# Issuing full matmuls as 32-column PE tiles in a fused attention and feed-forward kernel

## The chip, the cores and the metric

The kernel runs on one core of a Trainium2 chip. The metric is the device time of one execution in microseconds. The profile's span is about 1.8 us shorter than that time. "TensorE" is the matmul engine (PE in the profile, PEld its weight loads), VectorE is DVE, ScalarE is ACT, GpSimd is POOL.

## The reference

Eight batches of 12 heads, 448 tokens, head size 64, go through attention with one added to the softmax's denominator; the result, as 3584 rows of 768, goes through a feed-forward layer that takes the elementwise maximum of three up projections.

```python
scores = (1.0 / np.sqrt(64)) * np.matmul(q, k.transpose(0, 1, 3, 2))
m = np.max(scores, axis=-1, keepdims=True)
e = np.exp(scores - m)
attn = e / (np.sum(e, axis=-1, keepdims=True) + np.exp(-m) + 1e-09)
x = np.matmul(attn, v)            # then (8, 448, 12, 64) -> (3584, 768)
h = np.maximum(np.maximum(x @ w1, x @ w2), x @ w3)
out = h @ w_out
```

## The kernel before

Four heads make a group, three groups a batch. The groups' scores, exponentials and AV products are woven into the feed-forward pieces of the batch before, so that TensorE always has work. The first batch goes in halves of 224 query columns (`scores_half`, `av_half`, `up_half`), so that the feed-forward can begin early; all others use 448 columns. These are the matmuls that the change touches, and the AV product that it does not touch:

```python
def scores_visit(i, units):                        # L187; scores_half (L260) is the same with 224 columns
    ...
        for hh in range(2):
            nc.tensor.matmul(
                out=stp[:, hh, 0:S],
                lhsT=qkT[hh * D : hh * D + D, c * SC : c * SC + 128],   # 64 rows x 128 columns
                rhs=qkT[hh * D : hh * D + D, S : 2 * S],
                start=True, stop=True)

def up_piece(b, fc, i):                            # L325; up_half (L344) is the same with 224 columns
    ...
    for dc in range(NDC):
        nc.tensor.matmul(out=p_i[:, 0:S], lhsT=w_sb[i][:, dc, ts(fc, 128)],
                         rhs=xT[b][:, dc, :], start=(dc == 0), stop=(dc == NDC - 1))

def out_piece(bp, t, nh):                          # L366
    ...
    for fc in range(NFC):
        nc.tensor.matmul(out=op_ps[:, 0:NW], lhsT=hT[bp][:, fc, ts(t, 128)],
                         rhs=wout_sb[:, fc, ts(nh, NW)], start=(fc == 0), stop=(fc == NFC - 1))

# av_group (L216) and av_half (L286): already 32-column tiles, one head each
            for c in range(NCH):
                for hh in range(GH):
                    nc.tensor.matmul(out=bank[32 * hh : 32 * hh + 32, 0:S], lhsT=weights(hh, c),
                                     rhs=eT[:, hh, c, :], start=(c == 0), stop=(c == NCH - 1))
```

Each matmul call becomes two instructions, a weight load and a matmul (3148 of each in the profile of before). The loads of q, k, v and of the four weight matrices are issued by GpSimd; the weights and the first eight groups' inputs are fetched in the first 60 us.

The softmax here doesn't subtract the row's maximum and nothing guards it: scores larger than these inputs give would overflow.

## Time and profile before

| | before |
|---|---|
| time, median of 2 runs | 360.17 us (359.98 to 360.36) |
| span of the profiled run, mean granted clock | 358.9 us, 0.999 |
| TensorE busy | 95%, 3148 matmuls and as many weight loads |
| VectorE, ScalarE busy | 59%, 54% |
| chain that ended last | 91% of it matmuls |
| DMA engines' busy share, 18 to 62 us | 1.27 (mean of 16 engines; over 1 means packets overlap) |

"Busy" for TensorE uses modelled ends of matmuls, so the distance between starts is the better measure. Three views carry the argument, and the prediction shows their lines: the page, and two stretches of TensorE's timeline. A timeline line has the start in us, the length in us, the engine, the line of the kernel, the operation and its tiles, partitions times columns, and how many records were merged.

### The profile page before, as it was taken

To read this page: it belongs to the slowest core of one execution; us is meant where nothing else is said; L and a number is where in the kernel's file an instruction comes from. 1 tells how busy PE (TensorE), PEld (TensorE's weight loads), DVE (VectorE), ACT (ScalarE), POOL (GpSimd) and SP (SyncE) were. 2 spreads that over 40 slices of the span, in tenths; PEclk is the share of its full clock that TensorE was granted. 3 is DMA by queue.
4 is the path that set the end of the run, shared out by engine and by line. 5 is a ranking of instruction groups with operands and counts; after the bars stand their busy time and mean duration, and the time that the engine had idled before them with its cause. 6 is when DMAs were issued, how large, how long until landed. Compare 5 with 4: busy or idle time off the path is not lost.

```text
span 358.9 us, 7470 instructions
## 1 busy us (share of the span) xinstructions
PE 341.4 (95%) x3148; PEld 178.2 (50%) x3148; DVE 213.4 (59%) x430; ACT 192.7 (54%) x247; POOL 58.1 (16%) x90
## 2 busy tenths in 40 slices
PE   3879899999999999999999999999999999999994
PEld 2557777544444444444444544444445444445552
DVE  3334566676666666665657657656656655656553
ACT  3697567875563664663762863763764664630000
POOL 8424532220220220220220220220000000000000
PEclk9999999999999999999999999999999999999999
DMA  9999999489746964857739876759421540012006
GB/s 137 193 208 206 202 199 161 59 171 162 102 66 124 179 125 75 118 107 161 103 57 122 150 166 101 102 99 188 53 54 26 136 118 2 0 46 88 2 4 173
DMA packets 71617, 40.75 MB, mean 114 GB/s; under 512 B 33824, under 2 KB 66848, under 8 KB 71584
## 3 DMA queue, kind: packets, MB, share of 16 engines
q0 software_dynamic: 35072, 21.01, 42.9%
q1 hardware_dynamic: 36272, 19.05, 22.2%
q8 instruction: 24, 0.39, 0.4%
q10 hardware_dynamic: 240, 0.23, 0.2%
q14 instruction: 9, 0.07, 0.1%
HBM read 42.47 MB, written 11.01 MB: 149 GB/s over the span
## 4 chain that ended last, share of the span: by engine, by line
PE 91%; ACT 2%; DVE 2%; DMA 2%; issue 1%; POOL 1%; DVEq 0%; POOLq 0%
PE p_i L325 41%; PE op_ps L366 15%; PE av L216 15%; PE stp L187 11%; PE p_i L344 6%; DMA ld_k<-in_k_dram 2%; PE trT L157 2%; ACT eTh L269 1%; PE stp L260 1%; PE num L286 1%; PE den L286 1%; ACT rb L302 0%; DVE xT L308 0%; ACT lnd L298 0%; DVE qkT L162 0%
## 5 line engine op out<-in xcount | busy, mean ns | idle before, releaser
L196 ACT ACTIVATE eT<-stp 112x896 f16<-112x896 f32 x168 | 141.9, 912 | 109.3 <-PE stp L187 109.3
L335 DVE TENSOR_TENSOR hT<-hT,p_i 128x448 f16<-128x448 f16 x84 | 52.2, 622 | 43.5 <-PE p_i L325 43.5
L366 PE MATMUL op_ps<-w_130,hT 128*128 128x384 f16 x336 | 57.9, 327 | 0.0
L325 PE MATMUL p_i<-xT,w_127 128*128 128x448 f16 x252 | 54.7, 353 | 0.0
L325 PE MATMUL p_i<-xT,w_129 128*128 128x448 f16 x252 | 54.6, 353 | 0.0
L325 PE MATMUL p_i<-xT,w_128 128*128 128x448 f16 x252 | 54.6, 353 | 0.0
L89 POOL DMA_DIRECT2D ld_v<-in_v_dram x24 | 17.0, 709 | 177.0 <-PE stp L187 171.8
L366 PEld LDWEIGHTS <-hT 128*128 128x128 f16 x336 | 31.6, 98 | 25.1 <-issue 3.0
L187 PE MATMUL stp<-qkT 64*128 64x448 f16 x336 | 42.7, 353 | 0.0
L373 DVE TENSOR_SCALAR o_sb<-op_ps 128x384 f32<-128x384 f32 x56 | 31.1, 556 | 18.4 <-PE op_ps L366 18.4
L216 PE MATMUL av<-eT,ld_v 112*32 112x448 f16 x672 | 38.8, 353 | 0.0
L333 DVE CAST hT<-p_i 128x448 f16<-128x448 f32 x42 | 26.2, 625 | 20.8 <-PE p_i L325 20.8
L325 PEld LDWEIGHTS <-w_127 128*128 128x128 f16 x252 | 23.6, 98 | 25.2 <-issue 4.4
L325 PEld LDWEIGHTS <-w_129 128*128 128x128 f16 x252 | 23.9, 98 | 24.7 <-issue 3.3
L325 PEld LDWEIGHTS <-w_128 128*128 128x128 f16 x252 | 23.9, 98 | 24.7 <-issue 3.3
L231 DVE COPY num<-av 128x448 f32<-128x448 f32 x42 | 26.2, 625 | 8.8 <-PE av L216 6.0
L269 ACT ACTIVATE eTh<-stp 112x896 f16<-112x896 f32 x24 | 20.5, 912 | 12.7 <-PE stp L260 12.6
L216 PEld LDWEIGHTS <-ld_v 112*32 112x32 f16 x672 | 18.6, 97 | 16.5 <-issue 5.0
L240 DVE TENSOR_TENSOR xT<-num,rb 128x448 f16<-128x448 f32 x42 | 25.9, 617 | 0.0
L187 PEld LDWEIGHTS <-qkT 64*128 64x128 f16 x336 | 11.3, 94 | 24.6 <-issue 19.1
L226 DVE COPY den<-av 128x448 f32<-128x448 f32 x21 | 13.1, 625 | 16.1 <-PE av L216 16.1
L216 PE MATMUL av<-eT,ones_121 112*32 112x448 f16 x336 | 19.8, 355 | 0.0
(161 smaller groups left out, 225.6 us busy)
## 6 DMA issues: line engine op xcount, KB each, us to landing
ld_v<-in_v_dram POOLq DMA_DIRECT2D x24, 224.0 KB, 4.1
ld_q<-in_q_dram POOLq DMA_DIRECT2D x23, 224.0 KB, 5.1
ld_k<-in_k_dram POOLq DMA_DIRECT2D x23, 224.0 KB, 6.1
out_dram<-o_sb SPq DMA_DIRECT2D x8, 336.0 KB, 3.0
out_dram<-o_sb SPq DMA_DIRECT2D x8, 288.0 KB, 3.8
out_dram<-o_sb SPq DMA_DIRECT2D x8, 240.0 KB, 3.4
out_dram<-o_sb SPq DMA_DIRECT2D x8, 192.0 KB, 2.7
w_127<-in_moe_w_dram POOLq DMA_DIRECT2D x3, 384.0 KB, 11.9
```

The costliest lines, as they stand in the source:

```text
L187: nc.tensor.matmul(out=stp[:, hh, 0:S], lhsT=qkT[hh * D : hh * D + D, c * SC : c * SC + 128], rhs=qkT[hh * D : hh * D + D, S : 2 * S], sta ...
L196: nc.scalar.activation(out=st["eT"][:, 2 * pr : 2 * pr + 2, c, :], in_=stp[0:SC, :, 0:S], func=AF.Exp, scale=scale,)
L216: nc.tensor.matmul(out=bank[32 * hh : 32 * hh + 32, 0:S], lhsT=weights(hh, c), rhs=eT[:, hh, c, :], start=(c == 0), stop=(c == NCH - 1),)
L231: nc.vector.tensor_copy(out=num[:, hf], in_=col_tiled(lambda hh, c: v16[:, hh, c, hf::2])[:, 0:S])
L240: nc.vector.tensor_tensor(out=xT[b][:, 2 * g + hf, :], in0=num[:, hf], in1=rb, op=ALU.mult)
L269: nc.scalar.activation(out=st[key][:, 2 * pr : 2 * pr + 2, 2 * n : 2 * n + 2, :], in_=stp[0:SC, :, 0:S].rearrange("p h (c q) -> p h c q", ...
L325: nc.tensor.matmul(out=p_i[:, 0:S], lhsT=w_sb[i][:, dc, ts(fc, 128)], rhs=xT[b][:, dc, :], start=(dc == 0), stop=(dc == NDC - 1),)
L333: nc.vector.tensor_copy(out=dst, in_=p_i[:, 0:S])
L335: nc.vector.tensor_tensor(out=dst, in0=dst, in1=p_i[:, 0:S], op=ALU.max)
L344: nc.tensor.matmul(out=p_i[:, ts(j, HQ)], lhsT=w_sb[i][:, dc, ts(2 * fp + j, 128)], rhs=xT[b][:, dc, ts(half, HQ)], start=(dc == 0), stop= ...
L366: nc.tensor.matmul(out=op_ps[:, 0:NW], lhsT=hT[bp][:, fc, ts(t, 128)], rhs=wout_sb[:, fc, ts(nh, NW)], start=(fc == 0), stop=(fc == NFC - 1),)
L373: nc.vector.tensor_scalar(out=o_sb[:, ts(nh, NW)], in0=op_ps[:, 0:NW], scalar1=1.0 / LAMBDA, scalar2=None, op0=ALU.mult,)
```

## The change

The matmuls of five functions go through a helper that cuts the stationary operand into strips of 32 columns and issues one matmul for each strip. The output lands in the same place, in four strips of 32 partitions. The intent is to use one kind of column tile throughout, as the AV product does; the products to compute are the same. (`CT = 64`, used in one experiment, is this helper with another constant.)

```diff
+    CT = 32
+
+    def mm(out, lhsT, rhs, start, stop):
+        m = lhsT.shape[-1]
+        for j in range(0, m, CT):
+            nc.tensor.matmul(
+                out=out[j : j + CT],
+                lhsT=lhsT[:, j : j + CT],
+                rhs=rhs,
+                start=start,
+                stop=stop,
+            )
+
@@ scores_visit, scores_half, up_piece, up_half, out_piece
-                nc.tensor.matmul(
+                mm(
... (the same one-line edit in each of the five)
```

## The prediction

> **What bounds the kernel now.** I read the page from the top: busy shares, the slices, the chain that ended last, then the groups, and last the timeline of TensorE.

> ```profile
> PE 341.4 (95%) x3148; PEld 178.2 (50%) x3148; DVE 213.4 (59%) x430; ACT 192.7 (54%) x247; POOL 58.1 (16%) x90
> ...
> PE   3879899999999999999999999999999999999994
> ...
> PEclk9999999999999999999999999999999999999999
> ...
> q8 instruction: 24, 0.39, 0.4%
> ...
> PE 91%; ACT 2%; DVE 2%; DMA 2%; issue 1%; POOL 1%; DVEq 0%; POOLq 0%
> PE p_i L325 41%; PE op_ps L366 15%; PE av L216 15%; PE stp L187 11%; PE p_i L344 6%; DMA ld_k<-in_k_dram 2%; PE trT L157 2%; ACT eTh L269 1%; PE stp L260 1%; PE num L286 1%; PE den L286 1%; ACT rb L302 0%; DVE xT L308 0%; ACT lnd L298 0%; DVE qkT L162 0%
> ```

> TensorE is full from slice 5 (36 us) to the end, at full clock, and 91% of the chain is matmuls. VectorE (59%) and ScalarE (54%) have room. So what counts is the distance from one matmul's start to the next. It can't be read from the mean of a group (353 ns for a 448-column matmul, an end that is modelled); it is read from starts in the timeline:

> ```profile
> 151.35 1.30 PE L325 MATMUL p_i<-xT,w_129 128*128 128x448 f16 x6
> 152.48 2.19 PE L366 MATMUL op_ps<-w_130,hT 128*128 128x384 f16 x12
> ...
> 155.28 0.94 PE L216 MATMUL av<-eT,ones_121 112*32 112x448 f16 x16
> 156.05 1.85 PE L216 MATMUL av<-eT,ld_v 112*32 112x448 f16 x32
> ```

> Six full up-projection matmuls take 152.48 - 151.35 = 1.13 us, 188 ns each. The AV product is already written as 32-column tiles, four to a round (one per head): 16 of them take 156.05 - 155.28 = 0.77 us, 192 ns for a round of four. In the single records a round has its four starts 2 to 5 ns apart and the next round begins 189 ns after the first (the median over all rounds of AV; full matmuls of L325: 189 ns too). A round of four 32-column tiles costs what one full matmul costs. The first phase, which works in halves of 224 columns, says the same at half the length:

> ```profile
> 30.04 0.57 PE L286 MATMUL den<-eTh,ones_121 112*32 112x224 f16 x16
> 30.43 0.94 PE L286 MATMUL num<-eTh,ld_v 112*32 112x224 f16 x32
> 31.30 0.56 PE L260 MATMUL stp<-qkT 64*128 64x224 f16 x8
> 31.79 1.32 PE L344 MATMUL p_i<-xT,w_128 128*128 128x224 f16 x12
> 33.05 0.81 PE L260 MATMUL stp<-qkT 64*128 64x224 f16 x8
> 33.78 0.57 PE L286 MATMUL den<-eTh,ones_121 112*32 112x224 f16 x16
> 34.18 0.94 PE L286 MATMUL num<-eTh,ld_v 112*32 112x224 f16 x32
> 35.05 0.57 PE L157 MATMUL trT<-ident_102,qk_641 112*128 112x112 f16 x8
> ```

> 16 small ones from 30.04 to 30.43: 0.39 us, 97 ns a round; single records give 96 ns for a round of four and 96 ns for one full 224-column matmul of L344.

> [...] rounds of four overlap as above, and the first start after a change between the forms of L325, L187 and L216 comes about 285 ns after the last one, not 189, so a change costs about 95 ns. [...] The 32-column loads of AV show no cost: four of them hide in a round of 96 ns. [...] 24 packets, 0.39 MB, for some 6,300 instructions.

> **The change part by part.** It removes 1,740 full-width matmuls with their weight loads: 756 (L325), 336 (L366), 336 (L187), 216 (L344), 96 (L260). It puts four times as many in: 6,960. AV (1,008 and 288) and the 112 transposes stay. Matmuls go from 3,148 as recorded (3,148 by this sum) to 8,368, so loads and matmuls together from 6,296 to 16,736. The order of the work, the waits (on the first matmul of a chain only) and the other engines' instruction lists are the same in both kernels; I compared the lists.

> Array time. L325: 756 rounds, 189 ns against 189: 0. L366: 384 columns, 162 ns against 162 by the same rule, 336 rounds: 0. Scores: two heads already run side by side (starts 4 ns apart, pairs 189 to 199 ns apart), and become eight tiles in place of two; if they too overlap, each pair gains 6 more starts of about 3 ns only in its tail. The last of four starts some 10 ns after the first, so each chain ends 10 ns later for its reader; on a full TensorE this is no time, and where TensorE waits, in the first 36 us, some 30 such waits are 0.3 us. [...] Sum of the array's part: within 0.5 us of zero.

> Supply of instructions. This is where I chose. Each round now eats 8 instructions (4 loads, 4 matmuls) where it ate 2. I counted the starts of before in 10 us stretches and multiplied them: 120 to 320 us would need 9,080 instructions in 200 us, one per 22.0 ns; 20 to 60 us need 696, 696, 744 and 624, one per 14.5 ns; 60 to 80 us 554 and 478. What can TensorE's sequencer deliver? The lines of the first phase above show 16+32+8+12+8+16+32 = 124 matmuls, 248 instructions, between 30.04 and 35.05, without a gap that isn't a wait. [...] Call the delivery time r. A stretch that needs n instructions takes n times r if that is over its 10 us. Summing the excess:
> r = 14 ns or less: about 0.5 us.
> r = 16.7 ns [...]: 1.6 + 1.6 + 2.4 + 0.4 = 6 us, all in the first 60 us.
> r = 20 ns: 3.9 + 3.9 + 4.9 + 2.5 + 1.1 = 16 us.
> r = 25 ns: 35 us before 80 us and (12,208 x 25 ns - 270 us) = 35 us from 80 to 350 us, 70 us in all.
> Fetching the instructions themselves: 16,736 at 64 bytes are 65 blocks; one takes 0.9 to 1.5 us in the trace, and a block lasts 256 x 22 ns = 5.6 us (3.7 us in the first phase). If the next block is asked for at the start of this one, it comes in time.

> **Rivals.**
> (a) Nothing happens: the array is the bound[...]. For it: the AV chains, which are this very form, keep 189 and 96 ns to their last round, in runs of 96 instructions. [...] Time 360 to 361 us.
> (b) The sequencer becomes the bound in the half-column first phase only, where a round lasts 96 ns and needs 8 instructions in it (12 ns each): 366 to 376 us.
> (c) It becomes the bound everywhere: scores need 16 instructions in 189 ns, out rounds 8 in 162 ns (20 ns each), up rounds 8 in 189 ns (24 ns each). [...] Against it: inside a round, starts are 2 to 5 ns apart with loads between. 400 to 430 us.
> (d) Faster, since TensorE would change form less often. [...] some 120 changes of 95 ns would give 11 us back. Nothing in before shows it: 112x32 beside 64x128 pays the full 95 ns.
> (e) Eight score tiles that do not all overlap: if they ran as two rounds, 216 pairs (168 of 189 ns, 48 of 96) would cost 36 us more. Against it: the pairs of row tiles and the rounds of column tiles each overlap in before.

> **Range and chances.** I give (a) about half, (b) a quarter, (c) and (e) together 0.2, (d) 0.03. The 2% line is 7.2 us, so the slow end of (a) and the quick end of (b), up to r = 17 ns, still count as the same. The middle lies at r of about 16.7 ns, 366 us; the range reaches from (a) at its best, 359 us, to r of about 23 ns, 400 us. Faster 0.03, same 0.52, slower 0.45.

> **What would show it.** In the profile of after: rounds of up at 189 ns, out at 162 ns and scores at 189 ns with four or eight starts some 3 ns apart mean (a). Starts spread evenly, 2r apart, in the chains of the half phase alone, mean (b), and the first op_ps start, at 68.1 us now, comes later by what is lost; in all chains, (c). Scores at twice their length beside up rounds of 189 ns mean (e); first starts after a change of form at 189 and not 285 ns, (d). The instruction queue should show about 64 packets; if gaps of a microsecond stand before blocks, fetching is the bound, which I hold for unlikely. The prediction is wrong if the time leaves 359 to 400 us, and its reasoning is wrong, whatever the time, if the rounds at full supply are not 189 ns.

## The result, and the profile after

The changed kernel took 381.66 us (median of 2 runs, 380.27 and 383.06) against 360.17 us: slower, at a ratio of 1.060 (95% interval 1.043 to 1.077). Ratios here are the mean time of one kernel's fast runs over that of the other's in the same rounds, so they aren't quite the ratio of the medians quoted.

The page of the changed kernel, the same lines as were shown of before. All changed matmuls now have the helper's line, L135:

```profile
PE 349.2 (92%) x8368; PEld 201.7 (53%) x8368; DVE 213.6 (56%) x430; ACT 192.9 (51%) x247; POOL 58.1 (15%) x90
...
PE   3767577999999999999999999999999999999994
...
PEclk9998889999999999999999999999999999999999
...
q8 instruction: 65, 1.06, 1.2%
...
PE 86%; ACT 5%; issue 4%; DVE 2%; DMA 2%; POOL 1%; DVEq 0%; POOLq 0%
PE p_i L135 44%; PE op_ps L135 14%; PE av L229 13%; PE stp L135 11%; ACT eT L209 2%; DMA ld_k<-in_k_dram 2%; PE trT L170 2%; ACT eTh L282 2%; PE num L299 1%; PE den L299 1%; DVE xT L321 0%; DVE qk L156 0%; ACT rb L315 0%; ACT rb L250 0%; DVE qkT L175 0%
```

The counts are as worked out: 8368 matmuls, 65 instruction packets. From slice 8 on the row of TensorE is all nines, as before. The difference lies in slices 2 to 7, the first 66 us: TensorE has holes, and in slices 4 to 6 the granted clock falls (to 0.8 in the row PEclk). In the chain "issue" grows from 1% to 4%: time in which an engine waited for nothing that the profile shows. The view of waits (engine and line, what it waited for, us in total, times, longest) puts it on TensorE:

```profile
PE p_i L135 <- issue: 8.5, 5, 3.0
...
PE den L299 <- issue: 2.7, 1, 2.7
...
PE stp L135 <- issue: 0.8, 2, 0.5
...
PE trT L170 <- issue: 0.5, 1, 0.5
```

These are 12.5 us in nine waits for issue; in before the same view lists none. The timeline shows where they stand, in the middle of a chain of matmuls that has all its inputs:

```profile
33.15 0.95 PE L135 MATMUL p_i<-xT,w 128*32 128x224 f16 x31
35.28 0.64 PE L135 MATMUL p_i<-xT,w 128*32 128x224 f16 x17 [1.19 <-issue]
...
37.51 0.95 PE L135 MATMUL p_i<-xT,w 128*32 128x224 f16 x31
41.48 0.64 PE L135 MATMUL p_i<-xT,w 128*32 128x224 f16 x17 [3.02 <-issue]
```

```
block k  its first instruction  gap before it  packet of block k+1 starts   packet k+1 to block k+1's start
   3           23.44 us             0.78 us    27.12 us  (3.68 us later)      2.24 us
   4           29.36                2.07       32.95     (3.59)               2.33
   5           35.28                1.45       39.03     (3.75)               2.45
   6           41.48                3.28       45.10     (3.62)               2.30
   7           47.40                0.81       51.17     (3.77)               2.43
   8           53.59                2.97       54.73     (1.14)               not starved
   9           58.34                none       61.59     (3.25)               2.21
  10           63.80                2.16       64.93     (1.13)               not starved
```

So in these eight rows one block is fetched ahead: the packet of the next one starts only after TensorE has entered a block. It starts 3.6 to 3.8 us later in the first 50 us, 1.1 us later at 53.6 and at 63.8 us, and 3.25 us later at 58.3 us; from its start another 2.2 to 2.5 us pass until TensorE runs on. The view by windows shows what differs; the last three numbers of a line are the granted clock, the DMA engines' busy share and GB/s:

```profile
30.00:32.00 2.00, 2.00 (x52) 1.92 (x48) 0.63 (x1) 0.00 (x0) 0.86 (x2) 0.50 1.08 212
38.00:40.00 2.00, 0.46 (x19) 0.20 (x12) 0.02 (x1) 1.18 (x2) 1.40 (x2) 1.00 1.45 199
62.00:64.00 2.00, 0.20 (x9) 0.20 (x12) 0.00 (x0) 1.24 (x2) 0.00 (x0) 1.00 0.00 0
```

At 38 us the DMA engines are saturated (1.45) with the loads of weights and inputs; at 62 us they are idle. At 58 us, where the packet was late again, the share was 1.44 (58 to 60 us); from 54 to 56 us it was 0.25. What the packet waits for, no run shows. A block thus takes about 3.7 + 2.3 = 6.0 us while they are saturated, 23.5 ns an instruction, and 1.1 + 2.3 = 3.4 us while they are idle, 13.3 ns an instruction. Before used up a block in 7.4 to 10.5 us in that phase, so its fetches, whose packets start late as well (2.0 to 3.1 us after the block, up to 50 us), were hidden.

The first line shows the second loss. Three times, for 3.4 us each, the granted clock was 0.50: from 29.3, 43.0 and 53.2 us on, each within 1.5 us of the end of a gap of 2.1 us or more. The gap's length alone does not decide: after the gap of 2.16 us that ends at 63.80 us the clock stayed full. In the traces of before and after the clock holds one value for multiples of 3.41 us (3.41, 6.83, 10.24, 13.65, 320.85 and 341.33 us; the last piece of each trace apart). Counted on that grid, TensorE was busy for 1.24, 1.49 and 1.09 us in the stretch before these three falls, and for 1.86 us in the one from 60.03 to 63.44 us. Of the 201 stretches at full clock in which matmuls ran in these two traces, the three were the only ones with less than 1.86 us busy, and the only ones followed by a fall. From 29.36 us, 65 small matmuls (16.25 rounds of 96 ns, 1.6 us) took 3.3 us; the other two times cost 1.1 and 1.4 us by the same count.

The sum: I compared the starts of ScalarE's 246 activations, which are the same in both kernels. The changed kernel is 17.8 us behind by the 57th (65 us in before), and from there to its end only 1.8 us more, 19.6 us in all. The 17.8 us are 12.3 of the 12.5 us of waits (0.2 us come later) and some 4.2 us of lowered clock; the remaining 1.3 us I didn't attribute. The later 1.8 us are one late block at 232 us (0.65 us) and a steady drift of 1.2 us, which two experiments below place.

The steady part is otherwise what the array's arithmetic said. A stretch of the changed kernel:

```profile
168.44 2.45 PE L135 MATMUL p_i<-xT,w 128*32 128x448 f16 x48
170.72 2.22 PE L135 MATMUL op_ps<-w,hT 128*32 128x384 f16 x48
...
173.57 0.94 PE L229 MATMUL av<-eT,ones 112*32 112x448 f16 x16
174.33 1.84 PE L229 MATMUL av<-eT,ld_v 112*32 112x448 f16 x32
```

48 small matmuls, which stand for 12 full ones, take 170.72 - 168.44 = 2.28 us, 190 ns a round. The median of rounds inside chains is 189 ns (448 columns), 163 ns (384), 96 ns (224), and 199 ns for a pair of scores, to the nanosecond what full matmuls took.

### The profile page after: what moved, and what is told of

Read it like the earlier page. It is cut to its first block, busy times and chain, and to the rows that moved or that the text cites. A ratio compares the mean times of both kernels' runs of the same rounds, so it can differ in the third digit from the quotient of the medians.

```text
span 378.5 us, 17910 instructions
## 1 busy us (share of the span) xinstructions
PE 349.2 (92%) x8368; PEld 201.7 (53%) x8368; DVE 213.6 (56%) x430; ACT 192.9 (51%) x247; POOL 58.1 (15%) x90
## 4 chain that ended last, share of the span: by engine, by line
PE 86%; ACT 5%; issue 4%; DVE 2%; DMA 2%; POOL 1%; DVEq 0%; POOLq 0%
PE p_i L135 44%; PE op_ps L135 14%; PE av L229 13%; PE stp L135 11%; ACT eT L209 2%; DMA ld_k<-in_k_dram 2%; PE trT L170 2%; ACT eTh L282 2%; PE num L299 1%; PE den L299 1%; DVE xT L321 0%; DVE qk L156 0%; ACT rb L315 0%; ACT rb L250 0%; DVE qkT L175 0%
## 5 line engine op out<-in xcount | busy, mean ns | idle before, releaser
L135 PE MATMUL p_i<-xT,w 128*32 128x448 f16 (+1 forms) x3888 | 175.8, 336 | 9.2 <-issue 8.5
L135 PEld LDWEIGHTS <-w 128*32 128x32 f16 x3888 | 101.9, 98 | 81.4 <-issue 24.9
L135 PE MATMUL op_ps<-w,hT 128*32 128x384 f16 x1344 | 58.1, 327 | 0.0
L135 PE MATMUL stp<-qkT 64*32 64x448 f16 (+1 forms) x1728 | 52.8, 339 | 4.7 <-DVE qkT L175 2.9
L135 PEld LDWEIGHTS <-hT 128*32 128x32 f16 x1344 | 40.6, 97 | 16.2 <-issue 2.8
L135 PEld LDWEIGHTS <-qkT 64*32 64x32 f16 x1728 | 18.1, 92 | 31.6 <-issue 23.9
L229 PE MATMUL av<-eT,ones 112*32 112x448 f16 x336 | 19.7, 355 | 0.0
L89 POOL DMA_DIRECT2D ld_q<-in_q_dram x24 | 17.0, 707 | 4.0 <-DMA w<-in_moe_w_dram 1.4
L89 POOL DMA_DIRECT2D ld_k<-in_k_dram x24 | 16.8, 701 | 2.6 <-DMA w<-in_moe_w_dram 1.1
L248 ACT ACTIVATE lnd<-den,one_b 128x448 f32<-128x448 f32 x21 | 14.3, 679 | 4.3 <-DVE den L239 4.3
## 6 DMA issues: line engine op xcount, KB each, us to landing
w<-in_moe_w_dram POOLq DMA_DIRECT2D x9, 384.0 KB, 12.5
```

Of the source, the lines that this page charges most:

```text
L89: nc.gpsimd.dma_start(out=tiles[name][:, h0 : h0 + step].rearrange("p h c d -> p h (c d)"), in_=src[:, h0 : h0 + step],)
L135: nc.tensor.matmul(out=out[j : j + CT], lhsT=lhsT[:, j : j + CT], rhs=rhs, start=start, stop=stop,)
L248: nc.scalar.activation(out=lnd, in_=den, func=AF.Ln, bias=one_b)
```

## The experiments

Theory A, formed from this trace: the blocks of instructions come too slowly where the DMA engines are saturated. Rivals: B, TensorE's sequencer can't decode more than one instruction in some 20 ns, whatever the DMA engines do; C, the form itself costs a little in every round; D, the lowered clock is the cause and not a consequence.

Twelve kernels ran, in four lots, each beside runs of before on the same chip (medians of before there: 360.73, 361.12, 360.67 and 360.80 us).

### Only the first phase tiled

`half_only`: `scores_visit`, `up_piece` and `out_piece` call `nc.tensor.matmul` again; the two half functions keep `mm`.

```diff
-                mm(              # in scores_visit, up_piece, out_piece
+                nc.tensor.matmul(
```

> Only the two half-column functions of the first phase (scores_half, up_half) issue 32-column tiles. Theory A (instructions of TensorE come in blocks of 256; the next block is asked for when the last one is begun, and while the DMA engines are saturated a block takes about 6 us from the start of one to the start of the next, 23 ns an instruction): the loss lies where many instructions meet saturated DMA engines, so most of it stays: +12 to +17 us on before, with idle gaps of TensorE put down to issue at every 256th instruction. Theory B (the sequencer decodes too slowly, whatever the DMA engines do): the same place and about the same time, but the starts stretched evenly inside a block. Theory C (a round of 32-column tiles costs a little more everywhere): the loss follows the number of tiled matmuls, 312 of 1740, +4 us.

377.41 us (376.12 to 379.03, 4 fast runs), ratio 1.046 (1.042 to 1.050): +16.7 us. Its waits:

```profile
PE p_i L135 <- issue: 7.0, 4, 3.0
...
PE den L299 <- issue: 3.0, 1, 3.0
```

All breaks are again after 191 modulo 256 instructions. By the 57th activation it is 17.9 us behind the profiled run of before, and that stays 17.9 to 18.0 us to the last activation: no drift at all. Theory C's +4 us is out.

### Only the full-column work tiled

`full_only`, the complement.

```diff
-                mm(              # in scores_half, up_half
+                nc.tensor.matmul(
```

> Only scores_visit, up_piece and out_piece issue 32-column tiles; the first phase is as before. Theory A: the full-column work needs one instruction per 22 ns, and its blocks come in 3.4 us when the DMA engines are not saturated, so it is hidden but for small ends: +1 to +3 us. Theory B, with a sequencer slow enough to cost 18 us in the first phase (20 ns an instruction): out and score rounds would be bound, but the average is not: +1 to +4 us. Theory C: 1428 of 1740 tiled matmuls, +15 us.

362.56 us (361.70 to 366.10, 7 fast runs), ratio 1.004 (1.002 to 1.006): +1.8 us, with no wait put down to issue. 1428 of the 1740 tiled matmuls cost half a per cent, 312 cost the rest. It is where the instructions fall, not how many there are.

### Full-column scores alone, and up and out projections alone

`scores_only` keeps `mm` in `scores_visit` only, `ffn_only` in `up_piece` and `out_piece` only (the edit is the same one line in the other functions).

> Only the full-column scores (scores_visit) issue 32-column tiles: eight tiles of 64 rows in place of two of 128 columns. In the trace of the change the steady part lags before by 1.2 us more at its end than at its beginning. If the eight starts of a pair (about 3 ns apart) make each of the 63 visits end some 14 to 20 ns later, it is +1 us (ratio 1.002 to 1.004). If the lag belongs to the feed-forward or to single late blocks of instructions, 0 (ratio 0.999 to 1.001).

362.05 us against 360.67 us (22 and 43 runs), ratio 1.004 (1.002 to 1.006). In its trace the lag grows evenly, by 0.98 us between the activations that start at 56 and 310 us in before. With 63 visits of scores in 21 groups, that is about 16 ns a visit. The starts show where: inside a visit two pairs of scores stay 199 ns apart, as in before, but from the last pair to the first matmul of the up projection after it are 305 ns, where before has 285. The 20 ns more are the time between the first and the last of the eight starts.

> Only the full-column up and out projections (up_piece, out_piece) issue 32-column tiles. Rounds of four took as long as one full matmul in the trace of the change, so 0 to +0.5 us (ratio 0.999 to 1.002). If a round of four cost even 1% more, 756 x 1.9 ns + 336 x 1.6 ns = +2 us (ratio 1.005).

361.50 us, ratio 1.001 (0.999 to 1.004): no difference that 22 runs could show. Its trace is 0.4 us behind at the last activation, of which 0.25 us are one step at 251 us. So most of the drift of the change belongs to the scores.

### Fewer loads in the first phase

`before_now` and `after_now` fill the weights by a memset on GpSimd in place of loading them; the results are wrong on purpose. The pair is compared with each other.

```diff
-            nc.gpsimd.dma_start(out=w_sb[i][:, 2 * g : 2 * g + 2, :], in_=src)
+            nc.gpsimd.memset(w_sb[i][:, 2 * g : 2 * g + 2, :], 1.0 / 64.0)
```

> Control, wrong result on purpose: before with the four weight matrices filled by a memset in place of their 12 loads, so that the DMA engines carry less in the first 60 us. All theories: 355 to 361 us, as TensorE hardly waits for weights in before.

380.49 us (377.81 to 381.23, 4 fast runs): the control missed its expectation by 20 us. TensorE waits 23.1 us for VectorE's copies of q and k, most of it near the beginning, where before waits 6.5 us. The trace shows how: one copy of q, 0.3 us long in most places, lasts 14.5 us, from 7.3 to 21.9 us, while GpSimd runs nine of the memsets (8.4 to 21.7 us), and a copy of k lasts 4.0 us beside the last three. The phase that matters, from 30 us on, is undisturbed.

> Wrong result on purpose: after with the same memset of the weights, to be compared with before_now. Theory A: with the DMA engines no longer saturated from about 30 us on, a block of instructions takes about 3.4 us (13 ns an instruction) and most gaps go: after_now minus before_now is 3 to 8 us in place of 20 to 21. Theory B (decode): the instructions are the same, so the difference stays 17 to 21 us. Theory D (the lowered clock is the cause and not a consequence of the gaps): the clock still falls to 0.83 between 40 and 60 us and the loss stays.

389.65 us (388.07 to 391.54, 4 fast runs): 9.2 us more than its control, where the unaltered pair differs by 20 to 21 us; the runs of either kernel spread by 3.4 us. Less than half of the loss is left, though more than the 3 to 8 us that I expected. The trace tells why it is not less: the loads of q, k and v still saturate the engines from 54 to 62 us (shares of 1.17 to 1.44) and from 68 to 70 us (1.40), and there the packets again start 3.1 to 3.7 us after the block, and the two largest gaps are 2.4 and 2.7 us; between 46 and 52 us, where the share is 0.03, the blocks follow each other in 3.6 to 3.7 us with packets 0.9 to 1.1 us after the block. Its waits for issue, 6.7 us in place of 12.5, and the view of those six microseconds:

```profile
PE p_i L135 <- issue: 3.4, 5, 2.1
PE den L299 <- issue: 2.4, 1, 2.4
PE stp L135 <- issue: 0.9, 1, 0.9
...
46.00:52.00 6.00, 5.62 (x247) 4.63 (x240) 2.41 (x5) 3.54 (x6) 0.50 (x1) 1.00 0.03 5
```

The mean clock is 0.992 to 1.000 in the four runs. Theory B, which expected 17 to 21 us, is out. So is D: gaps appear here, and in the change from 23.4 us on, before any fall of the clock.

### The rate of instructions measured by itself

`burst` is before with matmuls on a scratch bank that wait for nothing, 512 in the first phase and 1024 at the end.

```diff
+    def burst(nb):
+        scratch = ps1.tile([128, 512], FP32, tag="bank1", name="burst")
+        for n in range(nb):
+            j = 32 * (n % 4)
+            nc.tensor.matmul(out=scratch[j : j + 32, 0:32], lhsT=ident16[:, j : j + 32],
+                             rhs=ident16[:, 0:32], start=True, stop=True)
```

> Before, with two stretches of matmuls on a scratch bank added, each matmul of 32 columns by 32, four column tiles in turn, nothing to wait for: 512 pairs of weight load and matmul (1024 instructions, 4 blocks) in the first phase, where the DMA engines are saturated, and 1024 pairs (2048 instructions, 8 blocks) at the very end, where they only write the last results. Theory A: inside a block the pairs come quickly, and there is an idle gap at every 256th instruction; a block lasts about 3.4 us at the end (13 ns an instruction, 27 us in all) and about 6 us in the first phase (23 ns, some 24 us in all). Theory B (decode, the same rate at all times): evenly spaced starts, 20 ns an instruction in both places, 41 us and 20 us.

The timeline of its two bursts:

```profile
27.52 1.21 PE L443 MATMUL burst<-ident 128*32 128x32 f16 x128 [4.55 <-issue]
33.72 1.23 PE L443 MATMUL burst<-ident 128*32 128x32 f16 x128 [4.99 <-issue]
39.91 0.97 PE L443 MATMUL burst<-ident 128*32 128x32 f16 x97 [4.97 <-issue]
...
381.60 1.19 PE L443 MATMUL burst<-ident 128*32 128x32 f16 x128 [2.43 <-issue]
385.33 1.22 PE L443 MATMUL burst<-ident 128*32 128x32 f16 x128 [2.54 <-issue]
388.78 1.22 PE L443 MATMUL burst<-ident 128*32 128x32 f16 x128 [2.23 <-issue]
392.78 1.23 PE L443 MATMUL burst<-ident 128*32 128x32 f16 x128 [2.78 <-issue]
```

The burst gives 128 matmuls with their loads, exactly one block, and then a wait. A block lasts 6.20 us in the first phase (24.2 ns an instruction) and 3.45 to 4.01 us at the end (13.5 to 15.7 ns). Inside a block the 256 instructions start within about 1.0 us (1.2 us less the length of the last matmul), 4 ns each, at the full clock (the blocks at 21.7 and 377.9 us) as at 0.50, to which the clock had fallen for most of both bursts. So the sequencer is far quicker than anything that this kernel asks of it (one in 12 ns in the half-column rounds), and what limits a long run of short instructions here is the fetch. One profiled run; its time, 408.37 us, has no meaning beside before.

### Two tiles in place of four

```diff
-    CT = 32
+    CT = 64
```

> The change with tiles of 64 columns in place of 32: two matmuls for each full one. Counted from the trace of before, the windows of 10 us from 20 to 60 us then need 424, 460, 428 and 376 instructions, one per 22 to 27 ns. Theory A: that is just about what saturated DMA engines deliver (23.5 ns): 0 to +5 us, one or two gaps. Theory B with 20 ns an instruction: 0. Theory C (the price of column tiling itself): half of the loss or more, +9 us or more.

364.06 us (364.02 to 368.07, 4 fast runs), ratio 1.012 (1.006 to 1.018): +2.9 us, inside the range of A and below C's. Its trace has no gap at a border of blocks. Of the lag of 3.4 us in its trace, 0.8 us are there by the 25th activation and 1.7 us come evenly after 65 us, more than with 32 columns. The starts account for the 1.7 us: inside a visit two pairs of scores are 213 ns apart, against 199 with 32 columns and in before, and there are 105 such distances, 1.5 us. Why 64 columns cost these 14 ns is open, and so are the 0.9 us between the 25th activation and 65 us.

### Saturated DMA engines where there were none

Extra loads of a weight third, never read, are added for each head group from the seventh on, to before and to the changed kernel. With three per group:

```diff
+        if i >= 6:
+            extra_loads(3)       # 3 x 384 KB into scratch tiles, four buffers
```

> Control: before with three more loads of a weight third (384 KB written each, never read) per head group from the seventh group on, so that the DMA engines are nearly saturated in the steady part as well. Theory A: before needs one instruction in about 50 ns, so its blocks come in time: 360 to 364 us, except for loads of q, k, v that come late.

> The change with the same extra loads. Theory A: where the DMA engines are saturated a block of 256 instructions takes 6.0 us against the 5.6 us in which the steady part uses it up[...]: after_dummy minus before_dummy is 30 to 45 us in place of 20, and gaps put down to issue appear after 90 us, where the change alone has almost none. Theory B (decode): the extra loads change nothing, the difference stays at 18 to 22 us. Theory C (form): the same, 18 to 22 us.

This pair is inconclusive as a time. The control itself went to 397.89 us (372.42 to 452.21, one fast run of 4), because the transposes of q and k came late (17.6 us of waits of the scores), so the dose was too strong; the changed kernel took 420.90 us (408.81 to 429.04, one fast run of 4). With two per group, `extra_loads(2)`:

> Control with two extra loads per head group in place of three, since three starved before itself of its transposed q and k. All theories: 360 to 368 us, no waits of TensorE put down to issue.

> The change with the same two extra loads. Theory A: in the steady part, where the change alone is starved once for 0.6 us, blocks now start late when the extra loads saturate the DMA engines: several more gaps at executed instruction 191 modulo 256, 3 to 15 us more of waits put down to issue, and after_dummy2 minus before_dummy2 of 23 to 35 us in place of 20. Theories B and C: 18 to 22 us, no new gaps.

The control was now as good as before: 361.03 us, ratio 1.001 (0.999 to 1.004). The changed kernel with the same loads took 389.01 us in its one fast run, 28 us more than its control; its other three runs, 395.48 to 412.43 us, are classed as slow. Its waits for issue after 90 us, where the change alone has 0.2 us:

```profile
PE p_i L135 <- issue: 2.4, 4, 1.2
PE op_ps L135 <- issue: 1.4, 1, 1.4
PE stp L135 <- issue: 0.8, 2, 0.6
```

The gaps stand at 191 modulo 256. Before each of the ten gaps of about 0.3 us or more after 90 us, the packet of the starved block had started 3.7 to 4.9 us into the block before it, and the DMA engines' share there was 1.07 to 1.38. The same loads that cost before nothing starve the changed kernel, as A says. From the fast runs, the difference to the control grew from 20 to 28 us; with one fast run the size is rough, and the new waits in its trace, 18.0 us for issue in all against 12.5, are 5.5 of the 8 us.

No version here beats the kernel before, and before has no wait for issue to remove.

## Why the prediction was right or wrong

The time, 381.66 us, lies inside the stated range of 359 to 400 us, 16 us above the predicted 366 us. The likeliest class named was "within 2%"; it is slower by 6%. That the range holds the time is partly luck: 381.66 us lies between the ranges of (b), 366 to 376 us, and (c), 400 to 430 us, and it came about by a cause that the prediction held for unlikely.

**Right: the array.** Rounds of up, out, half-up and scores take what was stated (189, 163 and 96 ns, and 199 ns for scores, within the 189 to 199 ns stated of before), a round of four 32-column tiles one full matmul's time, eight score tiles one pair's. Rivals (d) and (e) did not happen: after a change of form between scores and up the first start still comes 293 to 303 ns after the last one, and not 189. The narrow weight loads show no cost here: ffn_only is level with before (ratio 1.001). The size of the score term, "only in its tail", came out at 1.0 us in the trace of scores_only and 1.4 us in its time, where I had put the array's part within 0.5 us.

**Right: that supply would bind first in the half-column phase** and not in the steady part, by counting instructions per 10 us. half_only and full_only divide the loss so, and the steady part of the change lost 1.8 us in 300 us. The first start of op_ps moved from 68.1 to 85.8 us, by the 17.8 us lost, as stated.

**Wrong: what the supply is.** The prediction says of fetching: "If the next block is asked for at the start of this one, it comes in time", and it held gaps of a microsecond before blocks "for unlikely". This step failed. It took the 0.9 to 1.5 us for which a packet is in transfer as the whole latency. The runs showed 1.1 to 3.8 us before the packet starts and 2.3 us from its start to the next instruction, 3.4 us in all with idle DMA engines and 6.0 us with saturated ones. The assumed need of one block in 3.7 us lies between the two.

**Wrong: r as a constant of the sequencer.** The delivery r was treated as one number, and the 16.7 ns in the middle of the range was an assumption of mine that no run shows. Inside a block of the burst the sequencer delivers an instruction in 4 ns, and matmuls start 8 ns apart, so neither 16.7 nor 25 ns is a floor for its tiles; across blocks r is 13 to 16 ns (DMA engines idle in the change and in after_now; the end of the burst) or 23.5 to 24 ns (engines saturated in the change; the first phase of the burst). So neither (b) nor (c) describes the mechanism, though (b) has the place right: the starts are not spread evenly, they come in whole blocks with gaps. A rate of 23.5 ns up to 55 us in the prediction's own sum (696, 696 and 744 instructions, half of 624) would give 6.4 + 6.4 + 7.5 + 2.3 = 22.6 us, against 17.8 us measured, of which 4.2 us are clock and not supply; I can't say what makes the sum too large.

**Not foreseen: the clock.** The granted clock fell to 0.50 three times after gaps (of 2.1, 3.3 and 3.0 us), which cost some 4 us.

**A small slip.** The prediction has TensorE full from slice 5 (36 us) on; that slice of before reads 8, and full it is from slice 6. Nothing rests on it.

**The evidence from before that was overlooked.** Before's instruction packets start 2.0 to 3.1 us after their block in the first 50 us, and within about 1 us of it, or even before, from 72 us on. That was in the trace of before; it needed the packets' starts beside the instruction count, not only their length.

## What to carry to other kernels

Cutting a matmul into column tiles cost the array next to nothing here (about 1 us, at the scores), but it multiplies instructions (3148 matmuls became 8368), and those came by DMA, in the first phase one block of 256 ahead: divide the time in which the busiest stretch of one engine uses up 256 instructions by the time that a block takes in that stretch, which is 3.4 to 3.7 us here with idle DMA engines (busy share 0.00 to 0.04) and 6 us with saturated ones (over 1). Where that ratio is near one, issue fewer and larger instructions in exactly the stretches in which loads saturate the DMA engines; elsewhere the number of instructions was nearly free (full_only: +1.8 us for 1428 matmuls made four). The waits that the profile puts down to "issue" here, at a fixed remainder of the instruction count by 256 (191), were this.
